# Paired norms, groups of four features, four exponent scalings on GpSimd and a planner that shifts tasks, in a clustered-attention and two-MLP kernel

## The chip, the core and the metric

The kernel runs on one core of a Trainium2 chip. Its engines work side by side: TensorE (PE, with its weight loads PEld), VectorE (DVE), ScalarE (ACT), GpSimd (POOL) and the sync engine (SP), which here issues every DMA. The metric is the device time of one execution in microseconds. Before the change three runs gave 753.04, 753.65 and 754.53 us, with a median of 753.65 us.

## The reference

All arrays are float32. Attention (batch 2, 8 heads, 768 positions, head size 64) masks by cluster. Two MLPs on 1536 tokens follow (512 to 2048 to 512 features).

```
mask   = q_assign[:, :, :, None] == k_assign[:, :, None, :]     # argmax over 16 centroids
scores = where(mask, q @ k^T / sqrt(64), -1e9)
attn   = softmax(scores)
x      = (attn @ v), heads side by side                          # 1536 x 512
h = x @ w_in ; x = (h * sigmoid(h)) @ w_out                      # first MLP
h = x @ w_in2; x = (max(h,0) + alpha * min(h,0)) @ w_out2        # second MLP
```

## The kernel before

**Numbers.** Every matrix is split into a high and a low 16-bit part, and a product is made of three 16-bit products (high by high, high by low, low by high). Each split needs a power-of-two scale, and the scale needs a bound on the matrix's norm.

**Weights.** Each of the four weight matrices comes as 8 pieces of 128x1024 numbers, loaded through few raw buffers, so that a load waits until the piece before it in its buffer has been used. `to_f32` turns a piece of raw words into numbers that can be scaled: ACT shifts the low word (L903), ACT or POOL scales the high word (L908 or L911, by a letter of `EXP_ON`), DVE joins them (L914 and L917). The profile gives L907 for the ACT form of L908, since that is where its statement begins. For the first MLP `sum_sq_pe` then makes the squares on PE (8 products of 128x128, L952) and DVE takes the diagonal sum (L954). `all_sum` (L503) adds over the partitions with a product by ones, `pow2_scale` makes the scale (L445 to L453), and `split` writes the two parts (L929 on ACT, L930 on DVE).

**Attention.** There are 96 units, one for each head of each tile of 128 queries. `front` makes the scores on PE (L796 with the cluster mask, L800 with q and k), DVE scales them and finds the extreme (L810), ACT takes the exponential (L815) and rounds to the high part (L819), DVE makes the low part (L820), and a DMA transposes both (L826). Three units later `back` multiplies by v (18 products, L838). After the eight units of a tile, `x_done` scales the result on DVE (L864), POOL splits it (L867, L868), a DMA transposes it (L869).

**First MLP.** The tiles are put together in seven chunks of 1, 1, 2, 2, 2, 2 and 2 tiles (128 or 256 tokens). `layer1` makes the 16 blocks of 128 features of a chunk two at a time: 24 products (L1190) into half a PSUM bank or a whole one, tanh on ACT (L1197), DVE (L1198), ACT (L1201), DVE (L1202). Then come the output products (L1221) and their eviction (L1228). `dh_cols` holds the scale of the tanh (L1180).

**Second MLP.** It goes through its weights as above, but its norms are squares on ACT (L944). The products are L1410, L1434 and, for the output, L1477.

**The order of the work.** The Python code emits tasks in some order. `Plan` then models every instruction with a cost, a queue per engine and the dependencies, and lists them by priority. `improve` runs the list 60 times forwards and backwards with small noise and takes the shortest modelled schedule. `plan_order` fixes that order on all five engines, SP's DMA issues included. So each engine does its work strictly in the planned order, and an instruction that waits holds up everything behind it on its engine.

Of the kernel before, what the change touches and what calls it, by code (L numbers as in the profile page):

```python
# [34 lines left out]
K_SCALE_ON = ("aaaa", "pppa")  # L35
V_SCALE_ON = ("papa", "appp")
SPLIT = ("aaaaaaaa", "aaaaaaaa", "aaaaaaaa", "aaaaaaaa")
EXP_ON = ("aaaaaaaa", "aaaaaaaa", "aaaaaaaa", "aaaaaaaa")

OUT_LAG = 2  # L40
READERS = 6
PLAN_ROUNDS = 60
MASK = 2.0 ** 15
BIT23 = 2.0 ** 23


class Plan:
# [144 lines left out]

    def improve(self, rounds):

        noise = Random(1)
        found = [self.run(list(range(len(self.ins))))]
        back = self.mirror()
        for _ in range(rounds):
            back.run([noise.gauss(0, 0.1) - t for t in self.ended])
            found.append(self.run([noise.gauss(0, 0.1) - t for t in back.ended]))  # L200
        return min(found, key=lambda x: x[0])

    def run(self, prio):
        import heapq
# [125 lines left out]
def cluster_attention_silu_prelu(  # L330
# [626 lines left out]

    def in_tasks(w, raws, o_dst, kind, modes, mp):
# [14 lines left out]
        def conv(j):  # L973
            t = raw(j)[:, :, 1].bitcast(F32)
            to_f32(raw(j), t, mp[j])
            if w2:
                sum_sq(t, raw(j)[:, :, 0].bitcast(F32), ss[:, j:j + 1])
            else:
                sum_sq_pe(view(raws[j % len(raws)], BF16, PC, 4)[:, :, 3], ss[:, j:j + 1], kind)

        def scale(b):
            if not w2:
                for o in range(8 * b, 8 * b + 8):
                    assert o < 8 or (("k", 0, (o - 8) // 3) if o < 20 else ("v", 0, (o - 20) // 3)) in did
            both = range(2 * b, 2 * b + 2)
            tot = all_sum([[ss[:, j:j + 1] for j in both]] * 2, kind)
# [21 lines left out]
    def out_tasks(w, raws, o_ts, o_dst, m_in, kind, modes, mp):  # L1008
# [12 lines left out]
        def conv(j):  # L1021
            if not w2 and j < 6:
                for o in range(4 * j, 4 * j + 4):
                    assert ("k", 0, o // 6) in did
            t = view(o_ts[j], F32, PC)
            to_f32(raw(j), t, mp[j])
            if w2:
                sum_sq(t, raw(j)[:, :, 0].bitcast(F32), ss[:, j:j + 1])
            load(j + len(raws))
            if not w2:  # L1030
                sum_sq_pe(view(o_ts[j], BF16, PC, 2)[:, :, 1], ss[:, j:j + 1], kind)

        def scale():
            tot = all_sum([ss[:, j:j + 1] for j in range(NPC)], kind)
# [123 lines left out]
    def layer1(c):  # L1158
# [14 lines left out]
        first = t0 % T == 0  # L1173
        if c and first:
            nc.vector.tensor_scalar(dh, w1["in"].inv, x_inv[b], 0.5, op0=ALU.mult, op1=ALU.mult)
        for f in range(KF):
            j = f // 2
            wi = [in_block(o_w, f // 2 * 2 + ff) for ff in range(2)]
            if c == 0 and f % 2 == 0:
                nc.vector.tensor_scalar(  # L1180
                    dh[:, j:j + 1], w1["in"].inv[:, j:j + 1], x_inv[b], 0.5,
                    op0=ALU.mult, op1=ALU.mult,
                )
            if f % 2:
                hp = psum("l", 2, n)
                for ff in range(2):
                    i = 0
                    for kd in range(KD):
                        for a, bb in ((0, 0), (0, 1), (1, 0)):
                            nc.tensor.matmul(  # L1190
                                out=hp[:, ff], lhsT=wi[ff][:, a, kd],
                                rhs=mov(bb, kd), start=(i == 0), stop=(i == 3 * KD - 1),
                            )
                            i += 1
                th = view(o_tmp + 2 * KB * ring("t1", 2), F32, 2, n)
                gh, gl = g[:, f - 1:f + 1, 0], g[:, f - 1:f + 1, 1]
# [404 lines left out]
```

## Time and profile before

| what | us |
|---|---|
| median of three runs | 753.65 |
| profiled execution | 756.6 |
| its span (first to last instruction) | 754.8 |
| busy: PE, DVE, ACT, POOL | 663.7, 598.3, 482.2, 128.7 |

The busy time of PE contains stretches at half clock. The mean granted clock over the span is 0.964 of full speed. Busy shares are best read by stretch, because attention with the first MLP (up to about 440 us), the second MLP's weights (about 440 to 620 us) and its products (to the end) have different limits.

### The profile page before, as it was taken

To read this page: it belongs to the slowest core of one execution; us is meant where nothing else is said; L and a number is where in the kernel's file an instruction comes from. 1 tells how busy PE (TensorE), PEld (TensorE's weight loads), DVE (VectorE), ACT (ScalarE), POOL (GpSimd) and SP (SyncE) were. 2 spreads that over 40 slices of the span, in tenths; PEclk is the share of its full clock that TensorE was granted. 3 is DMA by queue.
4 is the path that set the end of the run, shared out by engine and by line. 5 is a ranking of instruction groups with operands and counts; after the bars stand their busy time and mean duration, and the time that the engine had idled before them with its cause. 6 is when DMAs were issued, how large, how long until landed. Compare 5 with 4: busy or idle time off the path is not lost.

```text
span 754.8 us, 17044 instructions
## 1 busy us (share of the span) xinstructions
PE 663.7 (88%) x7035; PEld 500.2 (66%) x7035; DVE 598.3 (79%) x1084; ACT 482.2 (64%) x779; POOL 128.7 (17%) x231
## 2 busy tenths in 40 slices
PE   0363568689999999999999999998899999999997
PEld 0243346579888888888888898874344677666643
DVE  4798998998888689858977856779899999966650
ACT  7886967978879568747866967878664442422111
POOL 4442021432234532102120020100000000000000
PEclk9995558999999999999999999999999999999999
DMA  7979998999999898888897932353300100001001
GB/s 230 307 196 288 331 216 132 172 196 172 195 181 209 147 168 137 135 153 146 149 152 124 279 76 97 129 199 140 112 1 0 56 2 1 1 1 56 1 0 56
DMA packets 237357, 100.86 MB, mean 134 GB/s; under 512 B 217312, under 2 KB 227552, under 8 KB 237280
## 3 DMA queue, kind: packets, MB, share of 16 engines
q1 hardware_dynamic: 237280, 99.78, 60.9%
q8 instruction: 55, 0.90, 0.5%
q14 instruction: 22, 0.18, 0.1%
HBM read 43.03 MB, written 3.15 MB: 61 GB/s over the span
## 4 chain that ended last, share of the span: by engine, by line
PE 46%; DVE 13%; DMA 6%; ACT 4%; issue 3%; POOL 2%; ACTq 0%; POOLq 0%
PE s L1477 11%; PE w L1190 10%; PE w L1221 9%; PE x L838 4%; PE w L1434 4%; DVE arena L930 3%; DMA arena<-in_moe_w_out_dram 3%; PE s L796 2%; PE s L800 2%; DMA arena<-in_moe_w_in_dram 2%; PE x L1434 2%; PE m L1434 2%; DVE arena L1300 1%; DVE arena L917 1%; DVE arena L914 1%
## 5 line engine op out<-in xcount | busy, mean ns | idle before, releaser
L1190 PE MATMUL w<-arena 128*128 128x256 f16 (+1 forms) x1272 | 152.7, 258 | 3.6 <-DMA arena<-arena 2.3
L1221 PE MATMUL w<-arena 128*128 128x256 f16 (+1 forms) x1296 | 154.1, 257 | 1.6 <-DVE arena L1198 1.1
L1477 PE MATMUL s<-arena 128*128 128x512 f16 x576 | 136.1, 379 | 1.4 <-DVE arena L930 1.4
L838 PE MATMUL x<-arena 128*128 128x64 f16 x1728 | 120.3, 196 | 7.3 <-DMA arena<-arena 7.3
L1190 PEld LDWEIGHTS <-arena 128*128 128x128 f16 x1344 | 109.7, 98 | 18.3 <-issue 6.7
L1221 PEld LDWEIGHTS <-arena 128*128 128x128 f16 x1344 | 110.2, 98 | 16.2 <-issue 2.1
L815 ACT ACTIVATE s<-s,stat 128x768 f32<-128x768 f32 x96 | 83.9, 873 | 56.0 <-DVE s L810 49.2
L810 DVE TENSOR_SCALAR_CACHE_REDUCE s<-s,stat 128x768 f32<-128x768 f32 x96 | 97.6, 1021 | 24.3 <-PE s L800 23.2
L838 PEld LDWEIGHTS <-arena 128*128 128x128 f16 x1728 | 97.5, 100 | 19.7 <-DMA arena<-arena 9.3
L820 DVE TENSOR_TENSOR arena<-s,arena 128x768 f16<-128x768 f32 x96 | 91.4, 953 | 13.0 <-ACT arena L819 12.6
L1477 PEld LDWEIGHTS <-arena 128*128 128x128 f16 x576 | 56.0, 98 | 61.1 <-issue 2.3
L796 PE MATMUL s<-arena 80*128 80x384 f16 x192 | 68.0, 354 | 12.6 <-DVE arena L820 11.1
L819 ACT ACTIVATE arena<-s 128x768 f16<-128x768 f32 x96 | 77.5, 809 | 1.7 <-DMA arena<-arena 0.3
L1434 PEld LDWEIGHTS <-arena 128*128 128x128 f16 x672 | 65.6, 98 | 17.3 <-issue 1.0
L1394 ACT ACTIVATE arena<-arena,stat 128x512 f16<-128x512 f32 x48 | 33.6, 717 | 66.1 <-DVE arena L1391 66.0
L800 PE MATMUL s<-arena 128*128 128x384 f16 x192 | 68.2, 355 | 0.0
L450 POOL TENSOR_SCALAR stat<-stat 128x1 int32<-128x1 int32 (+1 forms) x41 | 11.6, 286 | 307.0 <-DVE stat L445 210.1
L914 DVE SCALAR_TENSOR_TENSOR arena<-arena 128x1024 int32<-128x1024 int32 x32 | 39.1, 1222 | 22.6 <-ACT arena L907 22.4
L1434 PE MATMUL w<-arena 128*128 128x256 f16 x336 | 56.5, 273 | 0.0
L930 DVE SCALAR_TENSOR_TENSOR arena<-arena,stat 128x1024 f16<-128x1024 f32 x40 | 51.9, 1315 | 4.9 <-ACT arena L929 4.9
L903 ACT ACTIVATE arena<-arena 128x1024 int32<-128x1024 uint32 x32 | 37.0, 1155 | 26.8 <-DMA arena<-in_moe_w_in_dram 16.4
L929 ACT ACTIVATE arena<-arena,stat 128x1024 f16<-128x1024 f32 x40 | 45.7, 1171 | 11.7 <-POOL stat L450 4.4
(176 smaller groups left out, 1061.6 us busy)
## 6 DMA issues: line engine op xcount, KB each, us to landing
arena<-in_moe_w_in_dram SPq DMA_DIRECT2D x16, 1024.0 KB, 6.1
arena<-in_moe_w_out_dram SPq DMA_DIRECT2D x16, 1024.0 KB, 6.4
arena<-in_k_dram SPq DMA_DIRECT2D x8, 384.0 KB, 4.8
arena<-in_q_dram SPq DMA_DIRECT2D x6, 512.0 KB, 5.1
arena<-in_v_dram SPq DMA_DIRECT2D x8, 384.0 KB, 5.1
out_dram<-arena SPq DMA_DIRECT2D x12, 256.0 KB, 2.1
arena<-arena SPq DMA_TRANSPOSE x149, 4.2
arena<-in_centroids_dram SPq DMA_DIRECT2D x1, 32.0 KB, 2.9
```

The lines of the kernel that those rows point to most:

```text
L796: nc.tensor.matmul(out=sc[:, j, :hs], lhsT=qt2[0:D + C, h], rhs=kt2[0:D + C, h % 2, j * hs:(j + 1) * hs], start=True, stop=False,)
L800: nc.tensor.matmul(out=sc[:, j, :hs], lhsT=qt1[:, h], rhs=kt1[:, h % 2, j * hs:(j + 1) * hs], start=False, stop=True,)
L810: nc.vector.tensor_scalar(sc[:, :, :hs], sc[:, :, :hs], nd_cols[:, H * (n % 2) + h:H * (n % 2) + h + 1], None, op0=ALU.mult, op1=ALU.min, ...
L815: nc.scalar.activation(out=p, in_=p, func=ACTF.Exp, scale=-1.0, bias=bias, accum_out=sums[n % 2][:, h:h + 1])
L819: nc.scalar.activation(out=hl[:, 0], in_=p, func=ACTF.Copy)
L820: nc.vector.tensor_tensor(out=hl[:, 1], in0=p, in1=hl[:, 0], op=ALU.subtract)
L838: nc.tensor.matmul(out=x_ps[0][:, h], lhsT=pt[:, ph * T + t], rhs=vt[:, h % 2, t, vh], start=(i == 0), stop=(i == 3 * T - 1),)
L930: nc.vector.scalar_tensor_tensor(out=lo, in0=t, scalar=s, in1=hi, op0=ALU.mult, op1=ALU.subtract)
L1190: nc.tensor.matmul(out=hp[:, ff], lhsT=wi[ff][:, a, kd], rhs=mov(bb, kd), start=(i == 0), stop=(i == 3 * KD - 1),)
L1221: nc.tensor.matmul(out=acc, lhsT=wo[:, a, f % 2, dt * 128:(dt + 1) * 128], rhs=g[:, f, bb], start=(i == 0), stop=(i == 3 * KF - 1),)
L1434: nc.tensor.matmul(out=hp[:, ff], lhsT=a_[:, a, kd, at + 128 * ff:at + 128 * ff + 128], rhs=b_[:, bb, kd], start=(k == 0), stop=(k == 5),)
L1477: nc.tensor.matmul(out=acc[t], lhsT=g[:, q, a, t * 128:(t + 1) * 128], rhs=wo[:, bb, f % 2], start=(first and q == 0 and k == 0), stop=(la ...
```

## The change

There are four parts.

1. `sum_sq_pe` takes two pieces. It is called for every second piece of the first MLP's weights with 16 products into one PSUM bank and one diagonal sum. The eight L954 that are left stand for pairs, and `all_sum` adds half as many columns.
2. `layer1` works on `nf = 512 // n` feature blocks at once. That is four for the two chunks of one tile, and two as before for the others. `dh` is set for two columns at once.
3. The row of `EXP_ON` for the first MLP's output weights becomes "apapapap": every second piece has its high word scaled on POOL (L911) instead of ACT.
4. `improve` keeps its best priorities, and then tries 300 times to shift whole tasks (runs of instructions of one Python function). Each task is shifted with a chance of 0.03, by a normal number of width 2.5. A shift that makes the modelled schedule no longer is kept, and a backward and forward run is tried from there.

```diff
-EXP_ON = ("aaaaaaaa", "aaaaaaaa", "aaaaaaaa", "aaaaaaaa")
+EXP_ON = ("aaaaaaaa", "apapapap", "aaaaaaaa", "aaaaaaaa")
+SHIFT_ROUNDS, SHIFT_US, SHIFTED = 300, 2.5, 0.03
...
+        for _ in range(SHIFT_ROUNDS):
+            shift = [noise.gauss(0, SHIFT_US) if noise.random() < SHIFTED else 0.0 for _ in range(task[-1] + 1)]
+            tried = [t + shift[k] for t, k in zip(base, task)]
+            found = self.run(tried)
+            if found[0] <= best[0]:
+                best, base = found, tried
+                back.run([-t for t in self.ended])
+                tried = [-t for t in back.ended]
+                found = self.run(tried)
+                if found[0] < best[0]:
+                    best, base = found, tried
...
-    def sum_sq_pe(tb, ss, kind):
+    def sum_sq_pe(tbs, ss, kind):
         ps = psum(kind, 128)
-        for i in range(PC // 128):
-            c = tb[:, i * 128:(i + 1) * 128]
-            nc.tensor.matmul(out=ps, lhsT=c, rhs=c, start=(i == 0), stop=(i == PC // 128 - 1))
+        parts = [tb[:, i * 128:(i + 1) * 128] for tb in tbs for i in range(PC // 128)]
+        for i, c in enumerate(parts):
+            nc.tensor.matmul(out=ps, lhsT=c, rhs=c, start=(i == 0), stop=(i == len(parts) - 1))
...
+        nf = 512 // n
         for f in range(KF):
-            j = f // 2
+            j = f // 4 * 2
...
-            if f % 2:
-                hp = psum("l", 2, n)
-                for ff in range(2):
+            if f % nf == nf - 1:
+                hp = psum("l", nf, n)
+                for ff in range(nf):
...
-                th = view(o_tmp + 2 * KB * ring("t1", 2), F32, 2, n)
+                th = view(o_tmp + 2 * KB * ring("t1", 2), F32, nf, n)
```

The planner gives the whole program another order. Three places of it follow; the lines of the changed kernel have other numbers, which are named each time.

On DVE, just ahead of the first tile's `x_done`, this stood before (L864 is the result that the first chunk waits for).

```order
L996 TENSOR_REDUCE stat<-stat 128x1
L1208 TENSOR_SCALAR stat<-stat 128x1
L810 TENSOR_SCALAR s_65,stat<-s_65,stat 128x2x384
L914 SCALAR_TENSOR_TENSOR arena<-arena 128x1024
L820 TENSOR_TENSOR arena<-s_64,arena 128x768
L917 SCALAR_TENSOR_TENSOR arena<-arena 128x1024
L820 TENSOR_TENSOR arena<-s_65,arena 128x768
L810 TENSOR_SCALAR s_64,stat<-s_64,stat 128x2x384
L864 TENSOR_TENSOR arena<-x,stat 128x512
```

Now the same place on DVE reads as follows (L886 is L864, L832 is L810, L842 is L820, L936 and L939 are L914 and L917, L974 is L954).

```order
L936 SCALAR_TENSOR_TENSOR arena<-arena 128x1024
L469 TENSOR_SCALAR stat<-stat 128x1
L882 TENSOR_TENSOR stat<-stat 128x8
L939 SCALAR_TENSOR_TENSOR arena<-arena 128x1024
L842 TENSOR_TENSOR arena<-s_65,arena 128x768
L974 SCALAR_TENSOR_TENSOR arena,stat<-w_68,arena 128x128
L936 SCALAR_TENSOR_TENSOR arena<-arena 128x1024
L832 TENSOR_SCALAR s_65,stat<-s_65,stat 128x2x384
L886 TENSOR_TENSOR arena<-x,stat 128x512
```

From the program's start to this instruction DVE now has 11 score scalings instead of 12, 9 low parts L820 instead of 11, 14 joins L917 instead of 15, 6 diagonal sums instead of 14, and 4 settings of `dh` instead of 8.

On POOL, between the last one-hot of the keys and the first split of `x`, this stood before (L579 writes a one-hot, L450 and L453 make scales).

```order
L579 TENSOR_SCALAR arena<-arena 128x12x16 x2
L450 TENSOR_SCALAR stat<-stat 128x1
L453 TENSOR_SCALAR stat<-stat 128x1
L450 TENSOR_SCALAR stat<-stat 128x2
L453 TENSOR_SCALAR stat<-stat 128x2
L579 TENSOR_SCALAR arena<-arena 128x8x16
```

Now POOL has this there (L933 is the exponent scaling L911, L601 is L579, L472 and L475 are L450 and L453).

```order
L601 TENSOR_SCALAR arena<-arena 128x12x16 x2
L472 TENSOR_SCALAR stat<-stat 128x2
L933 TENSOR_SCALAR arena<-arena 128x1024
L475 TENSOR_SCALAR stat<-stat 128x2
L472 TENSOR_SCALAR stat<-stat 128x1
L475 TENSOR_SCALAR stat<-stat 128x1
L601 TENSOR_SCALAR arena<-arena 128x8x16
L933 TENSOR_SCALAR arena<-arena 128x1024 x2
```

Three of the four scalings stand ahead of the first split of `x`, and the fourth directly behind it.

On DVE, at the first features of the first chunk, this stood before (L1198 and L1202 are the two steps of a group).

```order
L1198 SCALAR_TENSOR_TENSOR arena<-arena,w_69 128x256
L445 TENSOR_SCALAR stat<-w_68 128x1
L1036 TENSOR_SCALAR stat<-stat 128x8
L820 TENSOR_TENSOR arena<-s_65,arena 128x768
L858 TENSOR_SCALAR stat<-stat 128x8
L1211 TENSOR_TENSOR stat<-stat 128x1
L1202 SCALAR_TENSOR_TENSOR arena<-arena 128x2x128
```

Now it reads as follows (L1225 and L1229 are L1198 and L1202, L952 is L930, the low part of an output weight).

```order
L1225 SCALAR_TENSOR_TENSOR arena<-arena,w_69 128x512
L952 SCALAR_TENSOR_TENSOR arena<-arena,stat 128x1024 x2
L832 TENSOR_SCALAR s_64,stat<-s_64,stat 128x2x384
L952 SCALAR_TENSOR_TENSOR arena<-arena,stat 128x1024
L842 TENSOR_TENSOR arena<-s_65,arena 128x768
L1225 SCALAR_TENSOR_TENSOR arena<-arena,w_69 128x512
```

The steps are twice as wide, and the output weights' splits come right behind the first of them. Up to the last L1202 of this chunk DVE has 23 score scalings instead of 26, 21 low parts L820 instead of 25 and 15 splits L930 instead of 16. On PE the first product of the next chunk has 8 products L796, 8 L800, 64 L838, 16 of 16 columns and 16 L1221 less in front of it.

## Rows read from the trace of the kernel before

**Rows 1.** Stretches: length, busy PE, PEld, DVE, ACT, POOL (instructions); clock, DMA, GB/s.
```profile
0.00:60.00 60.00, 19.33 (x238) 14.34 (x238) 43.83 (x108) 48.66 (x72) 28.88 (x64) 0.99 0.89 239
60.00:120.00 60.00, 33.93 (x372) 24.35 (x373) 55.98 (x115) 43.12 (x59) 10.62 (x16) 0.58 1.03 268
120.00:160.00 40.00, 32.19 (x530) 26.69 (x530) 36.60 (x75) 34.03 (x63) 10.57 (x17) 0.96 0.94 164
160.00:440.00 280.00, 277.24 (x3885) 240.94 (x3885) 224.81 (x458) 208.62 (x380) 68.19 (x107) 1.00 0.93 166
440.00:620.00 180.00, 171.23 (x1188) 113.56 (x1186) 152.32 (x195) 115.86 (x163) 10.12 (x26) 1.00 0.25 84
620.00:754.80 134.80, 129.82 (x826) 80.30 (x824) 84.76 (x138) 31.87 (x47) 0.34 (x2) 1.00 0.05 16
```

**Rows 2.** Waits of PE from 60 to 120 us: total, times, longest.
```profile
PE s L796 <- DVE arena L820: 9.2, 5, 4.9
PE m L693 <- POOL arena L579: 6.3, 2, 5.4
```

**Rows 3.** Timeline of PE: start, us, instruction, idle before.
```profile
106.83 1.17 PE L838 MATMUL x<-arena 128*128 128x64 f16 x18
...
120.11 1.33 PE L1190 MATMUL w<-arena 128*128 128x128 f16 x11 [2.31 <-DMA arena<-arena]
```

**Rows 4.** Timeline of DVE: first `x_done` and last feature step of the first chunk.
```profile
112.96 0.69 DVE L864 TENSOR_TENSOR arena<-x,stat 128x512 f32<-128x512 f32 x1
...
164.22 0.41 DVE L1202 SCALAR_TENSOR_TENSOR arena<-arena 128x256 f16<-128x256 f32 x1
```

**Rows 5.** Timeline of DVE, back to back: what each instruction takes of the queue.
```profile
84.79 1.22 DVE L917 SCALAR_TENSOR_TENSOR arena<-arena 128x1024 int32<-128x1024 int32 x1
85.93 0.95 DVE L820 TENSOR_TENSOR arena<-s,arena 128x768 f16<-128x768 f32 x1
86.80 1.01 DVE L810 TENSOR_SCALAR_CACHE_REDUCE s<-s,stat 128x768 f32<-128x768 f32 x1
...
87.73 0.28 DVE L954 SCALAR_TENSOR_TENSOR arena<-w,arena 128x128 bf16<-128x128 f32 x1
...
87.94 1.22 DVE L914 SCALAR_TENSOR_TENSOR arena<-arena 128x1024 int32<-128x1024 int32 x1
...
103.81 0.56 DVE L1180 TENSOR_SCALAR stat<-stat 128x1 f32<-128x1 f32 x4
```

**Rows 6.** Groups by shape on DVE: count, busy us, mean ns, idle before.
```profile
L1202 DVE SCALAR_TENSOR_TENSOR arena<-arena 128x512 f16<-128x512 f32 x40 | 29.5, 739 | 4.2 <-ACT arena L1201 4.1
L1198 DVE SCALAR_TENSOR_TENSOR arena<-arena,w 128x512 f32<-128x512 f32 x37 | 25.2, 682 | 3.0 <-ACT arena L1197 3.0
...
L1198 DVE SCALAR_TENSOR_TENSOR arena<-arena,w 128x256 f32<-128x256 f32 x16 | 6.6, 414 | 0.0
L1202 DVE SCALAR_TENSOR_TENSOR arena<-arena 128x256 f16<-128x256 f32 x16 | 6.6, 418 | 0.5 <-ACT arena L1201 0.5
```

**Rows 7.** Groups by shape on POOL: scalings by a number per partition.
```profile
L728 POOL TENSOR_SCALAR arena<-arena,stat 128x512 f32<-128x512 f32 x11 | 7.6, 695 | 0.9
...
L606 POOL TENSOR_SCALAR arena<-arena,stat 128x768 f32<-128x768 f32 x8 | 7.3, 907 | 0.3
```

**Rows 8.** Timeline of POOL.
```profile
35.74 1.95 POOL L637 TENSOR_TENSOR arena<-arena 128x768 f16<-128x768 f32 x1 [1.73 <-ACT arena L636]
...
44.88 0.35 POOL L579 TENSOR_SCALAR arena<-arena 128x192 f16<-128x192 f16 x1 [3.00 <-DVE arena L578]
...
60.93 1.32 POOL L579 TENSOR_SCALAR arena<-arena 128x192 f16<-128x192 f16 x1 [2.14 <-DVE arena L578]
```

**Rows 9.** Timeline of DVE beside those of POOL.
```profile
36.22 2.56 DVE L917 SCALAR_TENSOR_TENSOR arena<-arena 128x1024 int32<-128x1024 int32 x1
...
60.76 2.56 DVE L930 SCALAR_TENSOR_TENSOR arena<-arena,stat 128x1024 f16<-128x1024 f32 x2
```

**Rows 10.** The chain that ended last: start, us, what.
```profile
720.00 30.02 PE s L1477 x139
```

More of the change, by code (lines that the diff above doesn't have):

```diff
@@ L195, in improve @@
         noise = Random(1)
-        found = [self.run(list(range(len(self.ins))))]
+        best = self.run(list(range(len(self.ins))))
+        base = [float(n) for n in range(len(self.ins))]
         back = self.mirror()
@@ L199, in improve @@
             back.run([noise.gauss(0, 0.1) - t for t in self.ended])
-            found.append(self.run([noise.gauss(0, 0.1) - t for t in back.ended]))
-        return min(found, key=lambda x: x[0])
+            tried = [noise.gauss(0, 0.1) - t for t in back.ended]
+            found = self.run(tried)
+            if found[0] < best[0]:
+                best, base = found, tried
+        task, last = [], None
+        for i in self.ins:
+            name = i.debug.bass_funcname
+            task.append(task[-1] + (name != last) if task else 0)
+            last = name
+        for _ in range(SHIFT_ROUNDS):
[6 more added lines that the diff above has]
+                tried = [-t for t in back.ended]
+                found = self.run(tried)
+                if found[0] < best[0]:
+                    best, base = found, tried
+        return best
     def run(self, prio):
@@ L977, in conv @@
                 sum_sq(t, raw(j)[:, :, 0].bitcast(F32), ss[:, j:j + 1])
-            else:
-                sum_sq_pe(view(raws[j % len(raws)], BF16, PC, 4)[:, :, 3], ss[:, j:j + 1], kind)
+            elif j % 2:
+                sum_sq_pe(
+                    [view(raws[i % len(raws)], BF16, PC, 4)[:, :, 3] for i in (j - 1, j)],
+                    ss[:, j:j + 1], kind,
+                )
         def scale(b):
@@ L985, in scale @@
             both = range(2 * b, 2 * b + 2)
-            tot = all_sum([[ss[:, j:j + 1] for j in both]] * 2, kind)
+            tot = all_sum([[ss[:, j:j + 1] for j in (both if w2 else both[1:])]] * 2, kind)
             pow2_scale(tot, 2, 14 if w2 else 15, None, m.s[:, both[0]:both[0] + 2], m.inv[:, both[0]:both[0] + 2])
@@ L1029, in conv @@
             load(j + len(raws))
-            if not w2:
-                sum_sq_pe(view(o_ts[j], BF16, PC, 2)[:, :, 1], ss[:, j:j + 1], kind)
+            if not w2 and j % 2:
+                sum_sq_pe(
+                    [view(o_ts[i], BF16, PC, 2)[:, :, 1] for i in (j - 1, j)],
+                    ss[:, j:j + 1], kind,
+                )
         def scale():
-            tot = all_sum([ss[:, j:j + 1] for j in range(NPC)], kind)
+            tot = all_sum([ss[:, j:j + 1] for j in range(0 if w2 else 1, NPC, 1 if w2 else 2)], kind)
             pow2_scale(tot, 1, 15, None, s, m.inv)
@@ L1175, in layer1 @@
             nc.vector.tensor_scalar(dh, w1["in"].inv, x_inv[b], 0.5, op0=ALU.mult, op1=ALU.mult)
+        nf = 512 // n
         for f in range(KF):
-            j = f // 2
-            wi = [in_block(o_w, f // 2 * 2 + ff) for ff in range(2)]
-            if c == 0 and f % 2 == 0:
+            j = f // 4 * 2
+            if c == 0 and f % 4 == 0:
                 nc.vector.tensor_scalar(
-                    dh[:, j:j + 1], w1["in"].inv[:, j:j + 1], x_inv[b], 0.5,
+                    dh[:, j:j + 2], w1["in"].inv[:, j:j + 2], x_inv[b], 0.5,
                     op0=ALU.mult, op1=ALU.mult,
                 )
-            if f % 2:
-                hp = psum("l", 2, n)
-                for ff in range(2):
+            if f % nf == nf - 1:
+                hp = psum("l", nf, n)
+                for ff in range(nf):
                     i = 0
+                    wi = in_block(o_w, f - nf + 1 + ff)
                     for kd in range(KD):
@@ L1190, in layer1 @@
                             nc.tensor.matmul(
-                                out=hp[:, ff], lhsT=wi[ff][:, a, kd],
+                                out=hp[:, ff], lhsT=wi[:, a, kd],
                                 rhs=mov(bb, kd), start=(i == 0), stop=(i == 3 * KD - 1),
@@ L1194, in layer1 @@
                             i += 1
-                th = view(o_tmp + 2 * KB * ring("t1", 2), F32, 2, n)
-                gh, gl = g[:, f - 1:f + 1, 0], g[:, f - 1:f + 1, 1]
+                th = view(o_tmp + 2 * KB * ring("t1", 2), F32, nf, n)
+                gh, gl = g[:, f - nf + 1:f + 1, 0], g[:, f - nf + 1:f + 1, 1]
                 nc.scalar.activation(out=th, in_=hp, func=ACTF.Tanh, scale=dh[:, j:j + 1])
```

## The prediction

> **What bounds the kernel now.** I read the stretches first [rows 1]. From 160 to 440 us PE is busy 277.2 of 280 us and from 620 us to the end 129.8 of 134.8, all at full clock. In the tail a product of 512 columns takes 30.02/139 = 0.216 us [rows 10], which is 2371 columns a microsecond, so a shorter schedule has nothing to take there. The loss is elsewhere. Up to 60 us PE works 19.3 us. From 60 to 120 us it works 33.9 us at a granted clock of 0.58, which is mostly the lower of its two levels (1.2 GHz), after it had worked only a third of the time. From 120 to 160 us it still idles 40 - 32.2 = 7.8 us, and from 440 to 620 us 180 - 171.2 = 8.8 us.
>
> So the question is how early PE gets dense work. From 60 to 120 us DVE is busy 56.0 of 60 us and ACT only 43.1 [rows 1]. The waits of PE name DVE's L820 with 9.2 us and POOL's one-hot with 6.3 us, whose input DVE makes [rows 2]. DVE is the bound there. The first dense work is the first chunk of the first MLP. PE finishes the last head of tile 0 at 106.83 + 1.17 = 108.0 us [rows 3]. DVE comes to L864 only at 112.96 us, with its queue full in between [rows 4], and PE starts L1190 at 120.11 us after waiting 2.31 us for the transpose [rows 3]. That is 7.15 us behind L864. The eighth and last feature step of this chunk ends DVE's part at 164.22 us [rows 4].
>
> **The change part by part.** What an instruction takes of DVE's queue is the distance to the next start [rows 5]: L917 1.14 us, L820 0.87, L810 0.93, L954 0.21 (its accumulator read overlaps), L1180 0.56/4 = 0.14.
>
> Pairs of norms. There are 8 L954 fewer in all, 8 x 0.21 = 1.7 us of DVE, and all eight are gone ahead of the first L864. The 128 squaring products on PE stay.
>
> Fours of features. 16 L1198 and 16 L1202 of 256 columns (414 and 418 ns) become 8 and 8 of 512 (682 and 739 ns) [rows 6]. That is 13.3 against 11.4 us, 1.9 us less before the overlap of neighbours, say 1 us. They lie from 120 us on, half of them in the first chunk. The first group now needs 48 products instead of 24 before its tanh can start, but there are four round trips through ACT and DVE for a chunk instead of eight. Four L1180 fewer give 0.6 us.
>
> GpSimd. Four exponent scalings of 1024 columns leave ACT, which has 16.9 us free from 60 to 120 us [rows 1], so I count nothing for that. On POOL a scaling takes 695 ns for 512 and 907 ns for 768 columns [rows 7]. An estimate for 1024 from these is 907 + 212 = 1119 ns. POOL has time, being busy 10.6 of 60 us [rows 1]. But POOL and DVE get in each other's way. L917 took 2.56 us [rows 9] instead of 1.14, beside a POOL operation of 1.95 us [rows 8]. A one-hot scaling took 0.35 us alone and 1.32 us [rows 8] beside two L930 [rows 9]. So each moved scaling costs DVE between 0 and 1.12 us. I take the half, 0.56 us, since DVE's L810 and L820, which have a PSUM operand, are about as much of its work there as the joins are.
>
> The Trainium skill, "SBUF — State Buffer", section "SBUF: two separate sides", speaks against this part. By it the port pair that GpSimd and VectorE share is an exclusive lock: a VectorE operation with two SBUF inputs and a GpSimd operation that reads SBUF do not overlap, and the later one waits for the whole other one. The rows above agree with it. By that rule every scaling that meets a join costs its full 1.12 us, and if all four do, the sum below is 2.2 us smaller; if they fall beside L810 and L820 they cost nothing, and it is 2.2 us larger.
>
> The new order. Ahead of the first L864 there are also one L810, two L820 and one L917 less: 0.93 + 1.74 + 1.14 = 3.8 us. With 1.7 us for the norms and 0.6 us for L1180 that is 6.1 us. Three of the four scalings stand ahead of the first split of x, at half cost 1.7 us. So L864 comes 4.4 us earlier, at about 108.6 us, and the first L1190 at about 115.7 us. PE has by then 22 products L838 less behind it; at 1.17/18 = 0.065 us [rows 3] that is 1.4 us at the low clock, 0.7 us at the full one. Net gain at this point: 3.0 to 3.7 us.
>
> A second reckoning is at the end of the chunk's features. Ahead of it there are three L810, four L820 and one L930 less (2.8 + 3.5 + about 1.1, taking L930 like L917), the norms and L1180 (2.3) and 0.6 us of feature steps: 10.3 us. Four scalings at half cost take 2.2 us off, which leaves 8.1 us. But PE has less done by then: 8 + 8 products of 384 columns, 64 of 64, 16 of 128 and 16 of 16, some 12,500 columns or 5.3 us at the rate above. Net gain 2.8 us. Behind that point PE is full in both orders, so the gain stands to the end, if DVE is not late with what was put off. I take 3.5 us for the head, with bounds of 0.6 us (the second reckoning with whole scalings: 10.3 - 4.5 - 5.3 = 0.5) and 5.4 us (the first with none: 6.1 - 0.7).
>
> The stretch from 440 to 620 us has the same loads in the same order, limited by the chain of load, conversion and next load, which begins when attention frees its buffers and so moves with the head. PE idles 8.8 us there. A reordering can win or lose a few of these, and no row says which. I bound it by -3 and +3 us, a third of that idle time, and take 1 us gain, because the search weighs just such waits. The final 4 us behind the last product stay.
>
> Sum: 3.5 + 1.0 = 4.5 us. The profiled execution took 756.6 us, its span 754.8. From 756.6 it goes to 752.1 us. That run was 2.95 us above the median of the runs shown, so the forecast there is 753.65 - 4.5 = 749.1 us.
>
> **The rivals.**
>
> 1. More than that. If PE's holes from 120 to 160 us (7.8 us) take up what was put off, the 10.3 us of DVE's queue arrive whole: 753.65 - 10.3 = 743.4 us. For it speaks that PE idles there only for lack of work, and that the new features come in longer pieces. Against it, DVE is busy 36.6 of these 40 us [rows 1], so attention cannot run ahead.
>
> 2. Given back later. The scores that were put off (three L810, four L820) are still to be done, and in 160 to 440 us DVE is busy 224.8 of 280 us [rows 1]. If PE then waits for L820 as it did earlier, the head's gain goes there: 753.6 us. Against it, 55 us of DVE are free in that stretch and the last attention units stand at the same place of PE's work in both orders.
>
> 3. Slower through POOL. Mechanism: a scaling on POOL waits for a DVE operation (up to 1.14 us), then runs 1.12 us, and the join L914 that needs it stands in DVE's strict queue, with scores, L864 and the one-hots behind it. That is up to 2.26 us each, 9.0 us for four, against the 6.1 us ahead of L864: 2.9 us later, 756.6 us. It decides from 6.1/4 = 1.5 us a piece on. For it: the one-hot's 1.32 instead of 0.35 us and DVE's 56.0 busy of 60 us. Against it: a scaling can start as soon as its load has landed, and the shift of the low word on ACT goes beside it. The exclusive lock that the Trainium skill states ("SBUF — State Buffer", "SBUF: two separate sides") is what would make this case; the trace shows it in single instructions [rows 8, 9].
>
> **How the numbers follow.** I give the forecast 0.60, rival 1 0.13, rival 2 0.12 and rival 3 0.15. The forecast's own range is 746 to 752 us (head 0.6 to 5.4, later stretch within 3). The range for all reaches down to 743, where the whole of rival 1 begins, and up to 755, which takes in rival 2 and half of rival 3; about 2 in 10 lie outside. A measurement here tells about 0.2% (1.5 us) from no change. Faster by more than that, below 752.1 us, are nearly all of the forecast and rival 1: 0.73. Within it are rival 2 without its tails and a little of the forecast: 0.13. Slower is rival 3 less a little: 0.14.
>
> **What would show it.** L864's first start at 107 to 110 us instead of 112.96, and the first L1190 at 114 to 117 us. The granted clock from 60 to 120 us a little above 0.58, since dense work begins earlier. PE's idle time from 120 to 160 us below 7.8 us. The last score product of attention and the first load of the second MLP's weights 3 to 4 us earlier. If L864 is earlier but these are not, rival 2 holds. If L914 waits for POOL by more than 1.5 us a piece, rival 3 does. It would be wrong altogether if the first 60 us, which the new order also changes (the query is loaded and scaled ahead of the key), shifted the first scores by more than 2 us either way.

## The result and the profile after

Four runs of the changed kernel gave 746.44 to 749.51 us, median 747.89 us. The kernel before, run beside it, gave 753.35 us. The medians differ by 5.5 us. The ratio from the comparison of the runs is 0.9907, with an interval of 0.9879 to 0.9934, which is 7.0 us (5.0 to 9.1). The forecast was 4.5 us less, 749.1 us.

The profiled execution took 747.38 us, with a span of 745.6 us. The profiled one of before took 756.6 us, with a span of 754.8 us. It lies 3.25 us above the median given here, but within the medians of the same kernel beside the experiments (754.9 to 756.6 us). The two spans differ by 9.2 us, at the upper end of the interval, and no row says which part of that belongs to the single executions.

The stretches after, with the columns of [rows 1]:

```profile
0.00:60.00 60.00, 19.47 (x236) 14.83 (x237) 46.61 (x105) 49.48 (x73) 33.90 (x65) 0.97 0.94 253
60.00:120.00 60.00, 37.87 (x464) 28.54 (x464) 55.88 (x107) 41.66 (x58) 17.09 (x21) 0.66 1.03 268
120.00:160.00 40.00, 33.80 (x578) 29.61 (x576) 36.48 (x67) 33.03 (x59) 10.08 (x15) 0.96 0.92 168
160.00:440.00 280.00, 275.19 (x3802) 237.49 (x3799) 218.76 (x443) 206.39 (x371) 65.79 (x106) 1.00 0.94 163
440.00:620.00 180.00, 173.99 (x1183) 113.00 (x1182) 159.04 (x206) 115.19 (x158) 9.99 (x26) 1.00 0.23 84
620.00:745.60 125.60, 120.86 (x775) 75.12 (x773) 77.42 (x124) 29.79 (x44) 0.78 (x2) 1.00 0.05 18
```

From 60 to 120 us PE works 37.9 us instead of 33.9, at a granted clock of 0.66 instead of 0.58, still mostly the lower of the two levels (1.2 GHz). DVE is as full there as before (55.9 of 60 us).

A stretch that ends at a fixed time does not compare two kernels of which one is ahead. So I split the span another way: 160 us, plus the PE work that is left at 160 us, plus the idle time of PE after it. Before, then after, in the same view from 160 us to the end:

```profile
160.00:754.80 594.80, 578.28 (x5895) 434.81 (x5894) 461.89 (x789) 356.36 (x589) 78.65 (x135) 1.00 0.52 107
```

```profile
160.00:745.60 585.60, 570.03 (x5756) 425.60 (x5752) 455.21 (x771) 351.38 (x572) 76.56 (x134) 1.00 0.53 107
```

Work left falls from 578.3 to 570.0 us: 8.3 us are won by 160 us. Idle time after it is 594.8 - 578.3 = 16.5 us before and 585.6 - 570.0 = 15.6 us after, another 0.9 us. PE is at full clock there in both.

In the head (the time up to 160 us), PE's waits from 60 to 120 us (columns as in [rows 2]) name the low part of the scores with 4.1 instead of 9.2 us. The 6.3 us for POOL's one-hot are gone, but 3.7 + 2.6 = 6.3 us for two other steps of the cluster work, both on DVE, stand in their place (L594, a step in making the one-hot, and L719). The joins (L939), ahead of the squaring products, are named with 6.8 instead of 2.5 us:

```profile
PE w L972 <- DVE arena L939: 6.8, 4, 2.7
PE x L860 <- DMA arena<-arena: 4.8, 2, 3.0
PE s L818 <- DVE arena L842: 4.1, 6, 1.1
PE m L789 <- DVE arena L594: 3.7, 1, 3.7
PE m L789 <- DVE has L719: 2.6, 1, 2.6
```

The first scaling of scores on DVE, before:

```profile
38.96 1.01 DVE L810 TENSOR_SCALAR_CACHE_REDUCE s<-s,stat 128x768 f32<-128x768 f32 x1
```

The same after, and behind it the landmarks of [rows 4] (instructions whose start marks how far the work has come):

```profile
35.47 1.02 DVE L832 TENSOR_SCALAR_CACHE_REDUCE s<-s,stat 128x768 f32<-128x768 f32 x1
...
103.98 0.69 DVE L886 TENSOR_TENSOR arena<-x,stat 128x512 f32<-128x512 f32 x1
...
149.32 0.69 DVE L1229 SCALAR_TENSOR_TENSOR arena<-arena 128x512 f16<-128x512 f32 x1
```

The first `x_done` is 9.0 us earlier than in [rows 4], and the last feature step of the first chunk 14.9 us. On PE the first product of the first MLP, at 120.11 us in [rows 3], now reads:

```profile
112.98 0.72 PE L1217 MATMUL w<-arena 128*128 128x128 f16 x5
```

The shapes that answer [rows 6] have no rows of 256 columns any more:

```profile
L1229 DVE SCALAR_TENSOR_TENSOR arena<-arena 128x512 f16<-128x512 f32 x48 | 34.6, 728 | 3.5 <-ACT arena L1228 3.5
L1225 DVE SCALAR_TENSOR_TENSOR arena<-arena,w 128x512 f32<-128x512 f32 x45 | 30.6, 680 | 3.4 <-ACT arena L1224 3.2
```

The four scalings on POOL, in its timeline:

```profile
73.57 2.09 POOL L933 TENSOR_SCALAR arena<-arena 128x1024 f32<-128x1024 f32 x1
...
86.77 1.10 POOL L933 TENSOR_SCALAR arena<-arena 128x1024 f32<-128x1024 f32 x1 [2.38 <-DMA arena<-in_moe_w_out_dram]
...
90.82 2.16 POOL L933 TENSOR_SCALAR arena<-arena 128x1024 f32<-128x1024 f32 x1 [2.95 <-DMA arena<-in_moe_w_out_dram]
...
106.57 1.10 POOL L933 TENSOR_SCALAR arena<-arena 128x1024 f32<-128x1024 f32 x1
```

Two took 1.10 us, as estimated, and two took an extra microsecond. Yet the joins on DVE did not get longer (1.22 us each, group by shape, 60 to 125 us):

```profile
L939 DVE SCALAR_TENSOR_TENSOR arena<-arena 128x1024 int32<-128x1024 int32 x10 | 12.2, 1218 | 0.0
L936 DVE SCALAR_TENSOR_TENSOR arena<-arena 128x1024 int32<-128x1024 int32 x10 | 12.1, 1219 | 1.1 <-ACT arena L929 1.0
```

One other thing on DVE did: the four settings of `dh`, beside the scaling at 86.77 us. In a run of the same order below (e0_control) no scaling stands beside them. The trace of after, then that of the control:

```profile
87.15 1.12 DVE L1206 TENSOR_SCALAR stat<-stat 128x2 f32<-128x2 f32 x4
```

```profile
88.34 0.60 DVE L1224 TENSOR_SCALAR stat<-stat 128x2 f32<-128x2 f32 x4
```

The last score product of attention on PE, before and after, 8.65 us earlier:

```profile
423.61 0.33 PE L800 MATMUL s<-arena 128*128 128x384 f16 x1
```

```profile
414.96 0.33 PE L822 MATMUL s<-arena 128*128 128x384 f16 x1
```

The end of the chain is as dense as in [rows 10]: 26.13/121 = 0.216 us a product.

```profile
714.91 26.13 PE s L1504 x121
```

### The profile page after: what moved, and what is told of

Read it like the earlier page. It is cut to its first block, busy times and chain, and to the rows that moved or that the text cites. A ratio compares the mean times of both kernels' runs of the same rounds, so it can differ in the third digit from the quotient of the medians.

```text
span 745.6 us, 16972 instructions
## 1 busy us (share of the span) xinstructions
PE 661.2 (89%) x7023; PEld 498.6 (67%) x7023; DVE 594.2 (80%) x1048; ACT 475.6 (64%) x759; POOL 137.6 (18%) x235
## 4 chain that ended last, share of the span: by engine, by line
PE 44%; DVE 23%; DMA 11%; issue 9%; ACT 9%; POOL 2%; SPq 1%; ACTq 0%; DVEq 0%; POOLq 0%
PE s L1504 10%; PE w L1217 10%; PE w L1248 9%; DVE arena L952 4%; PE x L860 4%; DMA arena<-in_moe_w_in_dram 4%; DMA arena<-arena 3%; PE s L818 3%; PE s L822 3%; DMA arena<-in_moe_w_out_dram 3%; PE w L1461 2%; DVE arena L939 2%; DVE arena L936 2%; ACT arena L925 2%; DVE arena L1422 2%
## 5 line engine op out<-in xcount | busy, mean ns | idle before, releaser
L1248 PE MATMUL w<-arena 128*128 128x256 f16 (+1 forms) x1296 | 149.4, 258 | 3.1 <-DVE arena L1229 2.5
L1217 PE MATMUL w<-arena 128*128 128x256 f16 (+1 forms) x1272 | 145.7, 257 | 0.9 <-DMA arena<-arena 0.5
L1504 PE MATMUL s<-arena 128*128 128x512 f16 x576 | 142.7, 379 | 0.5 <-DVE arena L952 0.5
L1248 PEld LDWEIGHTS <-arena 128*128 128x128 f16 x1344 | 112.3, 98 | 18.6 <-issue 5.3
L1217 PEld LDWEIGHTS <-arena 128*128 128x128 f16 x1344 | 112.1, 98 | 15.3 <-issue 1.8
L832 DVE TENSOR_SCALAR_CACHE_REDUCE s<-s,stat 128x768 f32<-128x768 f32 x96 | 97.7, 1021 | 19.6 <-PE s L822 17.1
L842 DVE TENSOR_TENSOR arena<-s,arena 128x768 f16<-128x768 f32 x96 | 91.1, 952 | 16.3 <-ACT arena L841 16.1
L860 PE MATMUL x<-arena 128*128 128x64 f16 x1728 | 93.2, 196 | 7.5 <-DMA arena<-arena 7.1
L1504 PEld LDWEIGHTS <-arena 128*128 128x128 f16 x576 | 55.9, 98 | 54.7 <-issue 0.7
L860 PEld LDWEIGHTS <-arena 128*128 128x128 f16 x1728 | 80.0, 100 | 16.9 <-DMA arena<-arena 10.1
L1461 PEld LDWEIGHTS <-arena 128*128 128x128 f16 x672 | 65.7, 98 | 22.5 <-ACT arena L1363 0.9
L472 POOL TENSOR_SCALAR stat<-stat 128x1 int32<-128x1 int32 (+1 forms) x41 | 12.6, 310 | 337.5 <-DVE stat L467 233.8
L951 ACT ACTIVATE arena<-arena,stat 128x1024 f16<-128x1024 f32 x40 | 46.0, 1176 | 16.5 <-POOL stat L472 6.2
L936 DVE SCALAR_TENSOR_TENSOR arena<-arena 128x1024 int32<-128x1024 int32 x32 | 39.1, 1224 | 20.9 <-ACT arena L929 20.8
L952 DVE SCALAR_TENSOR_TENSOR arena<-arena,stat 128x1024 f16<-128x1024 f32 x40 | 52.2, 1327 | 4.0 <-ACT arena L951 4.0
```

The costliest lines, as they stand in the source:

```text
L832: nc.vector.tensor_scalar(sc[:, :, :hs], sc[:, :, :hs], nd_cols[:, H * (n % 2) + h:H * (n % 2) + h + 1], None, op0=ALU.mult, op1=ALU.min, ...
L842: nc.vector.tensor_tensor(out=hl[:, 1], in0=p, in1=hl[:, 0], op=ALU.subtract)
L860: nc.tensor.matmul(out=x_ps[0][:, h], lhsT=pt[:, ph * T + t], rhs=vt[:, h % 2, t, vh], start=(i == 0), stop=(i == 3 * T - 1),)
L952: nc.vector.scalar_tensor_tensor(out=lo, in0=t, scalar=s, in1=hi, op0=ALU.mult, op1=ALU.subtract)
L1217: nc.tensor.matmul(out=hp[:, ff], lhsT=wi[:, a, kd], rhs=mov(bb, kd), start=(i == 0), stop=(i == 3 * KD - 1),)
L1248: nc.tensor.matmul(out=acc, lhsT=wo[:, a, f % 2, dt * 128:(dt + 1) * 128], rhs=g[:, f, bb], start=(i == 0), stop=(i == 3 * KF - 1),)
```

## Experiments

Theory: the gain is made ahead of the first MLP, by DVE work that the parts take away and by an order that uses it. Rivals: the planner's new draw of an order does it whatever the parts are; the earlier query load at the start does it; the scalings on GpSimd cost a share of it. Every kernel was timed in five rounds beside the kernel before, whose median was 756.64 us beside e1 to e4, 754.93 us beside e0 and e8 to e10, and 755.60 us beside e5 to e7 and e11. So ratios are compared. The table has, for the profiled execution of each, the split used above (worked out from the stretches view).

| kernel | ratio (interval) | PE work left at 160 us | PE idle after | of it 430 to 610 us |
|---|---|---|---|---|
| before | 1 | 578.3 | 16.5 | 8.4 |
| after | 0.9907 (0.9879 to 0.9934) | 570.0 | 15.6 | 6.0 |
| e0_control | 0.9926 (0.9902 to 0.9950) | 572.0 | 13.3 | 4.9 |
| e1_shifts_alone | 0.9995 (0.9983 to 1.0008) | 576.9 | 17.0 | 7.0 |
| e2_parts_no_shifts | 0.9965 (0.9948 to 0.9982) | 575.6 | 17.7 | 7.4 |
| e3_before_seed2 | 1.0043 (1.0022 to 1.0063) | 580.1 | 18.1 | 9.7 |
| e4_after_seed2 | 0.9910 (0.9890 to 0.9931) | 573.2 | 16.8 | 6.6 |
| e5_single_norms | 0.9995 (0.9979 to 1.0011) | 574.2 | 17.5 | 9.2 |
| e6_twos | 0.9961 (0.9943 to 0.9979) | 575.8 | 15.9 | 5.8 |
| e7_exp_act_replanned | 0.9905 (0.9890 to 0.9920) | 572.3 | 14.5 | 6.9 |
| e8_exp_on_act | 0.9937 (0.9918 to 0.9957) | 572.6 | 15.0 | 5.6 |
| e9_exp_pool8 | 0.9916 (0.9896 to 0.9937) | 573.7 | 15.8 | 6.4 |
| e10_key_first | 0.9949 (0.9931 to 0.9966) | 571.3 | 16.5 | 5.2 |
| e11_more_shifts | 0.9948 (0.9929 to 0.9967) | 573.6 | 18.0 | 9.0 |

After and e0_control have the same order, so 0.9926 (5.6 us) is a second measurement of the change. Their two executions differ by 2.0 us in the work left and by 2.3 us the other way in the idle time. Differences of that size between two traces say nothing.

### Shifts alone, parts alone

**e1_shifts_alone** is the kernel before with only the planner's shifts (part 4).

```diff
+SHIFT_ROUNDS, SHIFT_US, SHIFTED = 300, 2.5, 0.03
...
+        for _ in range(SHIFT_ROUNDS):
+            shift = [noise.gauss(0, SHIFT_US) if noise.random() < SHIFTED else 0.0 for _ in range(task[-1] + 1)]
...
```

> The kernel before with the 300 task shifts and nothing else. Theory 'search' (the gain of 5.5 us is mostly the order that the shifts find): 4 us or more faster than before, below 749.5 us, and the first product of the first MLP earlier than 117 us (before 120.1, changed kernel 113.0). Theory 'work' (the gain is the instructions removed from DVE and ACT): within 1.5 us of before. Theory 'draw' (any new run of the planner lands anywhere within some 3 us): no fixed value, 750 to 756 us.

Measured: 0.9995, no change, with 1.4 us less work left at 160 us and 0.5 us more idle time behind it.

**e2_parts_no_shifts** is the changed kernel without the shifts.

```diff
-SHIFT_ROUNDS, SHIFT_US, SHIFTED = 300, 2.5, 0.03
+SHIFT_ROUNDS, SHIFT_US, SHIFTED = 0, 2.5, 0.03
```

> The changed kernel with no task shifts: paired norms, groups of four and the shared exponents under the planner's old 60 rounds. 'Work': 4 us or more faster than before, 747 to 749.5 us. 'Search': within 1.5 us of before or up to 2 us faster, since my own reckoning of the removed instructions is 1.7 + 0.6 + 1 us of DVE less up to 4.5 us of contention. 'Draw': between 750 and 756 us. If e1 and e2 both gain 2 to 3 us the parts add up and both theories hold in part.

Measured: 0.9965. The parts alone bring 0.35% (2.6 us), the shifts alone 0.05%, both together 0.93% (0.74% in the control). Neither theory's 4 us came. In these draws the two do not add up: the shifts found a gain only in the kernel that had the parts. Each of the two is a single draw, though, and the next runs show how far draws scatter.

### How much is the draw of the search

**e3_before_seed2** and **e4_after_seed2** are the two kernels with another seed of the planner's noise.

```diff
-        noise = Random(1)
+        noise = Random(2)
```

> The kernel before with another seed of the planner's noise: nothing in the work changes, only the order. 'Draw' wants a difference of 2 us or more in either direction. 'Search' and 'work' want less than 1.5 us, since 60 rounds of the same kind are tried.

> The changed kernel with another seed, so other shifts are tried and kept. 'Search' and 'work' both want about the changed kernel's time again, 746 to 750 us, with the first product of the first MLP before 116 us. 'Draw' wants a time that is 2 us or more off 747.9 us, perhaps no better than before.

Measured: 1.0043 and 0.9910. The changed kernel keeps its gain with another order, so it is no accident of one draw. Over all runs here, the five orders that were planned for kernels with pairs and fours have ratios of 0.9905 to 0.9965 (after, e2, e4, e7, e11), and the three for the kernel before 0.9995 to 1.0043 (before, e1, e3). But the kernel before loses 0.43% by the seed alone, as much as a part is worth. e3 is also a case that speaks against reading landmarks. In its DVE timeline the first `x_done` and the last feature step of the first chunk come 5.5 and 8.4 us earlier than in [rows 4]:

```profile
107.48 0.69 DVE L864 TENSOR_TENSOR arena<-x,stat 128x512 f32<-128x512 f32 x1
...
155.79 0.42 DVE L1202 SCALAR_TENSOR_TENSOR arena<-arena 128x256 f16<-128x256 f32 x1
```

Yet it is slower, and its stretch from 160 us has more work left, 580.1 against 578.3 us. So something else must have come later; what it was is not shown:

```profile
160.00:758.20 598.20, 580.11 (x5884) 434.40 (x5882) 462.11 (x791) 357.17 (x591) 80.14 (x138) 0.99 0.53 108
```

**e11_more_shifts** goes on from the changed kernel's order with 1500 tries instead of 300.

```diff
-SHIFT_ROUNDS, SHIFT_US, SHIFTED = 300, 2.5, 0.03
+SHIFT_ROUNDS, SHIFT_US, SHIFTED = 1500, 2.5, 0.03
```

> The changed kernel with 1500 task shifts instead of 300. 'Search' wants more of the same kind: 1 to 4 us faster than the changed kernel, 744 to 747 us. If the model has no more that the chip honours, it is within 1 us of it, or slower.

Measured: 0.9948, with an interval that overlaps that of after only at its edge. Its first 300 tries are the same, so its modelled schedule is no longer than that of after, and on the chip it is not faster: 0.4% slower than after, 0.2% slower than the control, which has the same order as after. The 1 to 4 us that were hoped for did not come. The idle time of PE from 430 to 610 us is 9.0 instead of 6.0 us. There PE waits most for the squares of the second MLP's norms on ACT (view of PE's waits from 430 to 610 us, columns as in [rows 2]):

```profile
PE s L525 <- ACT arena L966: 3.7, 3, 2.6
PE w L1437 <- DVE arena L1418: 2.6, 2, 2.3
```

Here the model's last tenths of a per cent are not the chip's.

### GpSimd's share

Three kernels keep the changed kernel's order and move only the scalings. **e0_control** fixes that order by the planned begin times and changes nothing else. **e8_exp_on_act** and **e9_exp_pool8** plan the eight scalings as the changed kernel does, and then run none or all of them on POOL.

The first edit is in all three, the second in e8 (a capital A is planned as POOL's and runs on ACT), the third in e9 (a capital P is planned as ACT's and runs on POOL).

```diff
-        return best
+        return best[0], self.by_time(base)
...
-EXP_ON = ("aaaaaaaa", "apapapap", "aaaaaaaa", "aaaaaaaa")
+EXP_ON = ("aaaaaaaa", "aAaAaAaA", "aaaaaaaa", "aaaaaaaa")
...
-EXP_ON = ("aaaaaaaa", "apapapap", "aaaaaaaa", "aaaaaaaa")
+EXP_ON = ("aaaaaaaa", "PpPpPpPp", "aaaaaaaa", "aaaaaaaa")
...
```

> The changed kernel once more, its instruction order on all engines the same as that of the changed kernel, written out by begin times. It is the control for the three kernels with it: 747 to 749 us, ratio to before 0.990 to 0.994. Any other result would mean that the write-out itself moves the time.

> The order of the changed kernel on every engine, with only the four exponent scalings put back from POOL to ACT at the place of their begin time. If POOL's scalings cost DVE what I took (half of 1.12 us each, 2.2 us in all) and that stands on the path, this is about 2 us faster than the control, 745.5 us, with the second and third L936 after it no longer beside a 2.1 us scaling. If ACT is the tighter one, it is slower by up to 4 x 1.1 = 4.5 us. If both have slack, it is within 1 us of the control. I expect the last.

> The order of the changed kernel with all eight exponent scalings of the first MLP's output weights on POOL instead of four. Rival 3 of the prediction (a scaling waits, then the join waits for it) wants a loss of 1.5 to 2.3 us a piece, 6 to 9 us over the control. The half price wants 2.2 us over it. If the scalings are hidden, it is within 1 us. The first x_done (103.98 us in the changed kernel) shows how much of it reaches DVE's queue.

Measured: 0.9937, 0.9926 and 0.9916 with none, four and eight scalings on POOL. No cost can be seen, neither rival 3's 6 to 9 us for eight nor the half price's 2.2 us for four more. The slight trend downwards lies within the intervals. The first `x_done` comes at 105.95, 105.48 and 105.55 us in the three. In the control's timelines one sees who pays when two meet. On DVE:

```profile
85.28 2.12 DVE L954 SCALAR_TENSOR_TENSOR arena<-arena 128x1024 int32<-128x1024 int32 x1
...
91.44 2.12 DVE L957 SCALAR_TENSOR_TENSOR arena<-arena 128x1024 int32<-128x1024 int32 x1
```

And on POOL:

```profile
85.22 1.12 POOL L949 TENSOR_SCALAR arena<-arena 128x1024 f32<-128x1024 f32 x1 [0.54 <-DMA arena<-in_moe_w_out_dram]
...
90.92 1.58 POOL L949 TENSOR_SCALAR arena<-arena 128x1024 f32<-128x1024 f32 x1 [4.58 <-DMA arena<-in_moe_w_out_dram]
```

At 85.22 us POOL starts 0.06 us ahead of the join, runs its 1.12 us, and the join takes 2.12 us instead of 1.22. In the trace of after (above) it was the other way round: POOL's scaling at 90.82 us, behind the join that had started at 90.77 us, took 2.16 us and the join 1.22:

```profile
90.77 1.22 DVE L939 SCALAR_TENSOR_TENSOR arena<-arena 128x1024 int32<-128x1024 int32 x1
```

The Trainium skill says the same in "SBUF — State Buffer", section "SBUF: two separate sides": whichever of the two starts first holds the port pair for its whole instruction, and the other blocks. The rows agree with it.

So on a join DVE loses 0.9 us when it comes second and nothing when it comes first: 0 us for four scalings in after (where the settings of `dh` paid 0.5 us instead), 2 x 0.9 = 1.8 us in the control. With eight the joins' means are 1320 and 1218 ns, about 10 x (1.320 - 1.219) = 1.0 us:

```profile
L954 DVE SCALAR_TENSOR_TENSOR arena<-arena 128x1024 int32<-128x1024 int32 x10 | 13.1, 1320 | 1.5 <-ACT arena L943 1.3
L957 DVE SCALAR_TENSOR_TENSOR arena<-arena 128x1024 int32<-128x1024 int32 x10 | 12.2, 1218 | 0.0
```

**e7_exp_act_replanned** leaves the scalings out of the change and plans anew.

```diff
-EXP_ON = ("aaaaaaaa", "apapapap", "aaaaaaaa", "aaaaaaaa")
+EXP_ON = ("aaaaaaaa", "aaaaaaaa", "aaaaaaaa", "aaaaaaaa")
```

> The changed kernel with all exponent scalings on ACT and its own search, to be read beside the kernel with the same edit in a fixed order. If POOL's share is worth anything once the planner may use it, this is 1 us or more slower than the changed kernel. If not, within 1 us or faster.

Measured: 0.9905, as after. The third part of the change is worth nothing that can be measured, by either way of taking it back. The first `x_done` of this kernel comes 5.8 us later than in after, and its time is the same:

```profile
109.75 0.68 DVE L886 TENSOR_TENSOR arena<-x,stat 128x512 f32<-128x512 f32 x1
```

### The start

**e10_key_first** holds the control's planned times, but has the key's load and squares ahead of the query's again, as before. In the cut below, the first lines put the query's squares behind the key's, and the last ones its load behind the key's and the centroids'.

```diff
+        if n == 0:
+            KEY_FIRST.append((x.ins.name, marks["k"]))
...
+        KEY_FIRST.append((l_q.ins.name, l_k.ins.name))
+        KEY_FIRST.append((l_q.ins.name, marks["cent"]))
```

> The changed kernel with the start of the kernel before: the first key load and its square are issued ahead of the query's, everything else by the begin times of the changed kernel. In the changed kernel the first score scaling on DVE starts at 35.47 us, before at 38.96. If the new start is what brings the 3.5 us, the first scaling goes back to 38 to 39 us, the first product of the first MLP from 113 to about 116 us, and the end is 2 to 3.5 us later than the control, 750 to 751.5 us. If the start is not on the path, the end stays within 1 us of the control.

Measured: 0.9949 against the control's 0.9926, with overlapping intervals. By the medians it is 1.7 us slower (751.02 and 749.30 us), between the two forecasts. The first scaling of scores goes back by 0.9 us only, from 35.60 us in the control, and not to the 38.96 us of before:

```profile
36.49 1.02 DVE L845 TENSOR_SCALAR_CACHE_REDUCE s<-s,stat 128x768 f32<-128x768 f32 x1
```

The work left at 160 us is 571.3 us, against 572.0 in the control. What this trace lacks is idle time behind it (16.5 against 13.3 us), where two executions of one order differ by 2.3 us. The test is weak, since it brought back a quarter of the shift that it was made for, and it does not price the loads' order.

The run with the second seed (e4) says more. Its first scaling of scores starts 0.5 us earlier than before, and it has the whole gain (0.9910). So the gain does not need the earlier start:

```profile
38.43 1.02 DVE L832 TENSOR_SCALAR_CACHE_REDUCE s<-s,stat 128x768 f32<-128x768 f32 x1
```

### One part taken out, planned anew

**e5_single_norms** is the changed kernel with a diagonal sum for each piece, **e6_twos** with two features a step everywhere.

```diff
-            elif j % 2:
-                sum_sq_pe(
-                    [view(raws[i % len(raws)], BF16, PC, 4)[:, :, 3] for i in (j - 1, j)],
-                    ss[:, j:j + 1], kind,
-                )
+            else:
+                sum_sq_pe(view(raws[j % len(raws)], BF16, PC, 4)[:, :, 3], ss[:, j:j + 1], kind)
...
```

```diff
-        nf = 512 // n
+        nf = 2
```

> The changed kernel with a diagonal sum for every piece again (16 L974 instead of 8) and its own planner search with shifts. My price for the pairs is 1.7 us of DVE ahead of the first x_done: 749.5 us, 1.7 us over the changed kernel. If the search finds room for them it is within 1 us of it.

> The changed kernel with feature groups of two in the chunks of one tile, as before, and its own search. My price for the fours was 1 us of DVE plus 0.6 us for the settings of the scale, which stay paired here: 748.5 to 749.5 us. But the last feature step of the first chunk came 15 us earlier in the changed kernel (149.3 instead of 164.2 us) where I had reckoned 8 us. If four round trips instead of eight are what made that, it goes back to 158 us or later here and the end to 750 us or more.

Measured: 0.9995 and 0.9961. Without pairs nothing is left of the gain, without fours less than half. The expectations priced the pairs at 1.7 us and the fours at 1.6 us; 0.88% is 6.6 us and 0.54% is 4.1 us. Both contain a fresh draw, which alone moved e3 by 0.43% and e11 by 0.2 to 0.4%. So pairs are probably worth something (0.88% is twice that), though how much of it is the order is not shown, and whether fours are worth anything stays open. The trace of e5 has its last feature step of the first chunk at 139.63 us, 24.6 us earlier than before, and 4.0 us less work left at 160 us; what it lacks against after is in the work left (4.2 us more, but 2.2 us against the control) and in the idle time from 430 to 610 us, 9.2 instead of 6.0 us:

```profile
139.63 0.68 DVE L1225 SCALAR_TENSOR_TENSOR arena<-arena 128x512 f16<-128x512 f32 x1
```

In e6, with eight round trips of two features, that last step comes at 141.75 us, also earlier than in after (149.32 us) and not at 158 us or later. So four round trips instead of eight are not needed for the lead, and again an earlier landmark stands in a slower kernel:

```profile
141.75 0.41 DVE L1229 SCALAR_TENSOR_TENSOR arena<-arena 128x256 f16<-128x256 f32 x1
```

## Why the prediction was right, and where its sizes were off

**The bound and the place: right.** PE is nearly as full from 160 to 440 us as before (275.2 instead of 277.2 of 280 us) and as full in the tail, and DVE as full from 60 to 120 us. 8.3 of the 9.2 us between the traces are won by 160 us. With the control's execution it is 6.3 of 9.5 us.

**The head: the right sign, too small.** The forecast took 3.5 us, with an upper bound of 5.4 us. The traces show 6.3 to 8.3 us, of which up to 3 us may belong to the one execution of before. The reckoning for L864 can be compared with DVE's own time ahead of it, before and then after (columns of [rows 1]):

```profile
0.00:112.96 112.96, 48.60 (x544) 34.97 (x545) 92.77 (x207) 86.77 (x121) 37.44 (x77) 0.79 0.96 262
```

```profile
0.00:103.98 103.98, 44.09 (x499) 32.25 (x500) 87.26 (x182) 80.11 (x113) 46.83 (x79) 0.81 1.01 276
```

- DVE is busy 5.5 us less ahead of L864. 6.1 us were counted, so the count of instructions moved held nearly.
- The scalings on POOL were priced at 1.7 us of DVE there. They cost 0.5 us in this trace, at the settings of `dh`, and nothing at the joins, since POOL came second where the two met. The prediction read the lock as a full 1.12 us of DVE for every scaling that meets a join, and left out that GpSimd can be the one that waits.
- DVE's idle time ahead of L864 was taken as unchanged. It fell from 20.2 to 16.7 us, 3.5 us less, 2.8 us of it in the first 60 us, where the scores begin 3.5 us earlier. 5.5 + 3.5 = 9.0 us, as measured. The prediction named a shift of the scores by over 2 us as what would make it wrong altogether. That was too strict: the run with the second seed has the gain without the shift.

The second reckoning, DVE's lead less the PE work put off, was the better form. The lead at the last feature step is 14.9 instead of 8.1 us. Less the 5.3 us that were put off this is 9.6 us, and 8.3 us are seen. Of the 6.8 us that the lead is larger, 1.7 us are POOL's price (2.2 us less the 0.5 us paid) and 3.5 us the idle time. The other 1.6 us I can't place. The lead by itself tells little: it is 24.6 us in e5 and 22.5 us in e6, and the work left at 160 us falls by 4.0 and 2.5 us there.

The clock was named, and not priced. PE's busy time over the whole span fell from 663.7 to 661.2 us for the same products (661.1 us in the control), so some 2.5 us of the 8.3 probably come from the clock of 0.66 instead of 0.58; no run moves the clock alone. The other 5.7 us are less idle time up to 160 us (74.6 against 68.9 us, from the stretches), 3.9 us of it from 60 to 120 us.

**The later part: the size right by luck, the make-up not.** 1.0 us was forecast and 0.9 us seen. It is the sum of a loss of 2.0 us from 160 to 430 us (idle 2.8, now 4.8 us; the largest wait is for the transpose of the probabilities) and a gain of 2.4 us from 430 to 610 us, with 0.6 us in the tail. So rival 2, given back later, holds in a small part. All of these are about as large as the differences between two executions of one order. Two readings of the prediction were a little off, without effect on its sum: its lower bound for the head is 0.6 us in one place and 0.5 us in its bracket, and the time behind the last product is 754.8 - 750.0 = 4.8 us and not 4 us.

**The rivals.** Rival 1 (743.4 us) went too far. By the trace of after the head came nearer to its 10.3 us than to the forecast, by the control's it did not, and its mechanism shows little: the holes from 120 to 160 us shrank by only 1.6 of their 7.8 us. Rival 3 is refuted: L936 waited 1.0 us for ACT's scaling and never for POOL's, and eight scalings instead of none showed no cost. Half price for each was wrong, since DVE's own loss is settled by who starts first.

**What would show it.** L864 and L1190 came earlier than the intervals that were given (103.98 and 112.98 us against 107 to 110 and 114 to 117). The clock rose, PE's idle time from 120 to 160 us fell from 7.8 to 6.2 us, the last score product was 8.65 us earlier instead of 3 to 4, and the first load of the second MLP's weights 6.9 us (416.45 before, 409.53 us after).

**What stays open.** The gain is 5.5 us by the medians and 7.0 by the ratio, 5.6 in the control, and the traces show 9.2; how the smaller figures split is known no more closely than these traces tell. Nor do the runs price pairs and fours singly, or part the work taken off DVE from the order that the search made of it, and no run tells what part of this order's head is the query's earlier load.

No run beat the changed kernel. The one without scalings on POOL (0.9905) equals it and is simpler.

## What to carry to other kernels

Where a search sets the order, compare versions by more than one draw: here a new seed moved the time by 0.43% and more tries by 0.2 to 0.4%, as much as one part of the change. Compare two orders by the work that is left at a fixed time on the engine that is full afterwards, and not by a landmark: one kernel reached its landmark 8.4 us earlier and was slower, and another reached one 5.8 us later and was as fast. Work taken off the engine that bounds a stretch paid 0.35% with the old search of the order and 0.74 to 0.93% with the longer one, in single draws, so a change of the work and one of its order are best tried together and apart.

## What the hardware showed unexpectedly

- A scaling on GpSimd of 128x1024 float32 numbers took 1.10 us by itself. Beside a join with two SBUF inputs on VectorE the one that started second took 0.9 to 1.1 us more (2.16 or 2.12 us), and the first none. A VectorE scaling of only 128x2 numbers, started behind one of them, took 0.74 instead of 0.22 us. Even eight scalings on GpSimd cost the kernel nothing that the runs can see.
- Two executions of the same order differed by 2 us in how far PE had come at 160 us, and made it up later: 745.6 and 745.3 us of span.
